# Two planning numbers of a conv and mixer kernel: the second group's convolution counted at 1.2 times its VectorE time, and the decoding of the second token weight put three tenths ahead

## The chip, the cores and the metric

The kernel runs on one core of a Trainium2 chip. The metric is the device time of the program in microseconds. Its engines are called here as the profile calls them: PE (TensorE, matmuls; PEld its weight loads), DVE (VectorE), ACT (ScalarE), POOL (GpSimd) and SP (SyncE, which issues DMAs).

## The reference

Eight batches of 4096 tokens by 192 channels go through a causal convolution of 7 taps, with softmaxed taps for each of 8 heads of 24 channels, and then through a mixer: an MLP over the tokens (4096 to 256 to 4096) and an MLP over the channels (192 to 1536 to 192), each with a residual sum.

```python
w = exp(weight - max); w = w / (sum(w) + 1e-09)          # (8 heads, 7 taps)
x = einsum('hk,bskhg->bshg', w, windows_of_7(x))         # causal, zeros ahead
h = maximum(x^T @ w_tok1, 0) @ w_tok2                    # token mix, for each batch
u = x + h^T
out = u + maximum(u @ w_ch1, 0) @ w_ch2                  # channel mix, for each token
```

The token weights come as pairs of 32-bit words (the two halves of 64-bit floats), so they are decoded on the chip.

## The kernel before

**Groups and tiles.** `GROUPS` has five groups of batches: [0], [1], [2,3], [4,5], [6,7]. While the channel part of one group runs in 8 tiles of 512 tokens, the next group's convolution and first token mix run beside it as background. This document numbers the tiles of group 0 from 0 to 7. In one tile PE does, in program order: `channel1` (L959: six pairs of 18 matmuls into two PSUM tiles, L932; ACT makes `hh` at L971 and DVE `hl` at L972 out of each), `mix2` of the next tile (L861, L862; two DVE sums for each of 4 pieces), half of `channel2` (L1006, L1007), `transposed` of the next tile (L892, copies on ACT L894 and DVE L895), and the other half of `channel2`.

**The background of group 0.** Four lists of items (streams), all of `group=1`:
- the convolution of batch 1 (`stage1(1)`): for each of four quarters of the tokens (`q2`), loads (L621), 8 first taps on ACT (L631) and 48 later taps on DVE (L633), two heads to an item; 96 DVE items in all. A quarter ends with a store on POOL (L657);
- its first token mix (`mix`, L721): 8 items of 4 matmuls for each quarter, which may start when that quarter is convolved;
- the decoding of `w_tok2` (`decode_items`): 12 jobs, each a 512 KB load on SP (L206), an ACT step (L170), four DVE steps (L172, L173, L176, L179), an ACT copy (L185) and a DVE difference (L186). Four jobs make one quarter of `t2s`, which `mix2` of two tiles reads;
- the stores of `t2s`: for each quarter 8 ACT copies into `stage` (L1109, two buffers) and 4 DMAs on SP (L1111) to `t2d`, where later groups read it. Its last item, `through` (L1090), opens the pool for the convolution of group 2 and starts that (`stage1(2)`), with the first of its two halves of channels only; the other half's pool opens after tile 6.

**The planner** (`Background`, L35). The order of all engines is written out while the program is built. Each piece of foreground calls `fg(pe, dve, after)`: it moves a planned PE clock on by `pe` ns, puts background items in until the planned DVE clock is `after` (200 or 600 ns) ahead, and books `dve` ns of foreground. An item moves the planned DVE clock by its `cost`: 660 ns for a pair of taps of batch 1, 3083 ns in all for a decode job. Of the streams whose first item is ready, `fill` (L64) takes the one with the smallest key:

```python
ready = [s for s in ready if s["items"][0].pe]      # once self.dve >= self.pe + until
self.pop(min(ready, key=lambda s: s["done"] / s["total"] - s["lead"]))   # L82
```

So a stream with a lead of 0.1 is kept 0.1 of its own total ahead of one without. Items of cost 0 (loads, ACT steps, stores) also wait while the DVE clock is full. Mix items are left out inside `channel1` (`tiled`). `require` (L94), called before each `mix2` of group 0, puts in whatever of the decoding that tile still needs, and then sets the planned PE clock up to the planned DVE clock. `finish` (L105), called for group 1 at the head of tile 7, puts in all that is left of its four streams.

Of the kernel before, what the change touches and what calls it, by code (L numbers as in the profile page):

```python
# [34 lines left out]
class Background:  # L35
# [9 lines left out]
        self.pe = 0.0  # L45
        self.dve = 0.0

    def add(self, items, lead=0.0, group=None):
        total = sum(it.cost for it in items) or 1.0
        self.streams.append(dict(items=items, total=total, done=0.0, free=self.pe, lead=lead, group=group))  # L50

# [63 lines left out]
def conv_mixer_kernel(ctx: ExitStack, tc: tile.TileContext, x, weight, w_tok1, w_tok2, w_ch1, w_ch2, out):  # L115
# [16 lines left out]
    TT = TJ * P  # L132
# [3 lines left out]

    AHEAD = {1: 5, 2: 3}
    LAST = NJ // MJ - 3
    ST = RB * P

    def f32(ap):
        return ap.bitcast(F32)
# [7 lines left out]
    bg = Background()  # L150
# [94 lines left out]
    def t2_job(q2, a0, na, kc=None):  # L245

        c0 = q2 * ST + a0
        cs = slice(2 * c0, 2 * (c0 + na))
# [22 lines left out]
    def decode_items(dec, jobs, loaded=False):  # L271


        n = dec.n / 0.96
        sts = [{} for _ in jobs]
        items = []

        def add(cost, lag, fn, tag=None, gate=None, eager=False):
            items.append(Item(fn, cost + (190 if cost else 0), lag, gate=gate, tag=tag, eager=eager))

        def load(i):
            def fn():
                jb = sts[i]["jb"] = jobs[i][0]()
                sts[i]["raw"] = jb.get("raw") or dec.load(jb["src"], jb["shape"])

            if i < len(jobs):
                add(0, 0, fn, eager=True)

        def begin(i):
            def fn():  # L290
                sts[i]["a"] = dec.a(sts[i], sts[i]["jb"].get("top", lambda: None)())

            if i < len(jobs):
                add(0, 12e3 if i == 0 and not loaded else 0, fn, eager=loaded and i == 0)

        def high(i):
            if not jobs[i][4]:
                return

            def fn():  # L300
                jb = sts[i]["jb"]
                hi, lo = jb["make"]() if "make" in jb else (jb["hi"], jb["lo"])
                sts[i]["b"] = dec.b(sts[i], hi, lo, jb.get("view", lambda v: v))

            add(0, 0, fn, gate=jobs[i][3])

        def low(i):
            def post():
                if "post" in sts[i]["jb"]:
                    sts[i]["jb"]["post"]()  # L310

            if jobs[i][4]:
                add(n, 0, lambda: sts[i]["b"][0](), jobs[i][1])
            add(0, 0, post, jobs[i][1])
            items.extend(jobs[i][2])

        load(0)
        load(1)
        begin(0)
        for i in range(len(jobs)):  # L320
            if i:
                high(i - 1)
            for k, c in enumerate((0.5, 0.5, 1, 1)):
                add(n * c, 500 if k == 0 else 0, lambda i=i, k=k: sts[i]["a"][k]())
                if k == 0 and i:
                    low(i - 1)
                if k == 2:
                    begin(i + 1)
            load(i + 2)
        high(len(jobs) - 1)  # L330
        add(0, 500, lambda: None)
        low(len(jobs) - 1)
        return items
# [264 lines left out]
    def stage1(gi, pools):  # L598
        bs = GROUPS[gi]
        nb = len(bs)  # L600
        convolving, mixing, accs = [], [], []
# [10 lines left out]
        def load(q2, part):  # L612
# [3 lines left out]
            for i, b in enumerate(bs):  # L616

                at = (b * S + q2 * ST - HALO) * D + ds.start
                assert at >= 0
# [40 lines left out]
        def t1_load(n):  # L660
            q2, q = divmod(n, RB // MJ)
            js = slice(q * MJ, (q + 1) * MJ)

            def part(d):
                return d[q2 * ST:(q2 + 1) * ST].rearrange("(p j) t m -> p j t m", j=RB)[:, js]

            top = t1d.rearrange("s (t m) -> s t m", t=1)
            if nb == 1:
                t1 = mp.tile([P, MJ, 1, JT], F32, name="t1", bufs=AHEAD[nb] + 1)
                nc.sync.dma_start(out=t1, in_=part(top))  # L670
            elif gi == 2:
                if n < LAST:
                    t1 = mp.tile([P, MJ, 2, JT], F32R, name="t1", bufs=AHEAD[nb])
                else:

                    if "spare" not in done:
                        done["spare"] = mp.tile([P, 2, ND, TT], F32R, name="other").rearrange("p a c t -> p (a c t)")
                    w = MJ * 2 * JT
                    t1 = done["spare"][:, (n - LAST) * w:(n - LAST + 1) * w].rearrange("p (j t m) -> p j t m", t=2, m=JT)
                nc.sync.dma_start(out=f32(t1[:, :, 1:2]), in_=part(top))  # L680
            else:
                t1 = mp.tile([P, MJ, 2, JT], F32R, name="t1", bufs=AHEAD[nb])
                nc.sync.dma_start(out=f32(t1), in_=part(t1p))
            states[q2]["t1", q] = t1
            mark("t1", n)
# [5 lines left out]
        def t1_lo(q2, q):  # L691
# [3 lines left out]
            nc.gpsimd.dma_start(  # L695
                out=t1p[q2 * ST:(q2 + 1) * ST].rearrange("(p j) t m -> p j t m", j=RB)[:, js], in_=f32(t1)
            )
# [61 lines left out]
        def multiply(*a):  # L759
# [7 lines left out]
            for kc in range(KC):  # L767
# [3 lines left out]
                mixing.append(it)  # L771
            if n + AHEAD[nb] < (LAST if gi == 2 else NJ // MJ):
                mixing.append(Item(lambda: t1_load(n + AHEAD[nb])))
            if gi == 2 and n % 2 and n // 2 < NJ // MJ - LAST:
                mixing.append(Item(lambda: t1_load(LAST + n // 2)))

# [25 lines left out]
            bg.finish(gi)  # L802
            mix1_done(gi, accs)

        bg.add(convolving, group=gi)
        bg.add(second, group=gi)
        return start, finish

# [5 lines left out]
    def t2s_of(q2):  # L814
        if q2 not in t2s:
            t2s[q2] = t2sp[q2 % 2].tile([P, KC, 2, ST], F32R, name="t2s")
        return t2s[q2]
# [234 lines left out]
    td = decode_ctx.enter_context(tc.tile_pool(name="td", bufs=1, side="right", reuse_waits="tile"))  # L1052
# [5 lines left out]
    def first_items():  # L1058

        jobs, stores = [], []  # L1060
        state = {}

        def decoded(q2):
            state["t2", q2] = max(bg.pe, bg.dve)

        def stored(q2):
            state["stored", q2] = bg.pe

        decoded(0)
        for q2 in range(NS):  # L1070
            for kc in range(KC):
                for r in range(2):
                    a = (q2, kc, r)
                    stores.append(Item(lambda a=a: store_t2(*a, 0), lag=1000, gate=lambda q2=q2: state.get(("t2", q2))))
                    stores.append(Item(lambda a=a: store_t2(*a, 1), lag=600))
                    stores.append(Item(lambda a=a: store_t2(*a, 2), lag=1200))
            stores.append(Item(lambda q2=q2: stored(q2)))
            for a0 in range(0, ST, TT) if q2 else []:
                for kc in range(KC):
                    after = []  # L1080
                    if a0 + TT == ST and kc == KC - 1:
                        after.append(Item(lambda q2=q2: decoded(q2)))

                    def gate(q2=q2):
                        if q2 > 1 and (mixed[0] <= 2 * (q2 - 2) or ("stored", q2 - 2) not in state):
                            return None
                        return 0.0

                    jobs.append((lambda a=(q2, a0, TT, kc): t2_job(*a), ("t2", q2, a0 // TT), after, gate, True))
        def through():  # L1090

            decode_ctx.close()
            conv_pool(0)
            starts[2] = stage1(2, lambda k: cps[k])

        stores.append(Item(through))
        bg.add(decode_items(Decoder(td, TT, 2, 2), jobs), lead=0.1, group=1)
        bg.add(stores, group=1)

    t2p = []  # L1100
# [1 line left out]
    def store_t2(q2, kc, r, step):  # L1102

        if step == 0:
            t2p.append(td.tile([P, 2 * TT], F32R, name="stage", bufs=2).rearrange("m (j p) -> m j p", j=RB))
        if step < 2:
            js = slice(step * RB // 2, (step + 1) * RB // 2)
            v = f32(t2s[q2][:, kc, r]).rearrange("m (p j) -> m j p", j=RB)
            nc.scalar.copy(out=t2p[-1][:, js], in_=v[:, js])  # L1109
        else:  # L1110
            nc.sync.dma_start(out=t2d[q2][:, kc, r], in_=f32(t2p[-1]))  # L1111

    def conv_pool(k):
        cps[k] = ctx.enter_context(tc.tile_pool(name=f"cp{k}", bufs=1, reuse_waits="tile"))

    def run_ahead(gi):

        if gi and gi + 2 < len(GROUPS) and gi + 2 not in starts and bg.idle():
            starts[gi + 2] = stage1(gi + 2, lambda k: cps[k])
# [101 lines left out]
```

## Time and profile before

| | us |
|---|---|
| median of 3 runs (lowest, highest) | 2064.48 (2064.27, 2065.81) |
| the profiled execution's own time | 2064.22 |
| its span in the trace | 2062.5 |
| PE busy (weight loads) | 2051.7 (1898.3) |
| DVE busy | 1402.8 |
| ACT busy | 760.2 |
| granted PE clock, share of full | 1.0 |

The page's first part gives each engine's busy time, the second the same in 40 slices of the span. PE is at nine tenths or more in all of them, DVE in the third to the fifth of them (about 100 to 260 us) too; in the last third of the span DVE is at four to five tenths. A busy PE is not PE at its peak, so tiles are compared by the time from the first matmul of one `channel1` to that of the next: such stretches, and what each engine does in them, come from the view by windows.

### The profile page before, as it was taken

How to read it: one execution, taken by the hardware profiler on the slowest of the kernel's cores; microseconds unless marked ns; L12 is line 12 of the kernel's file. 1: busy time of each engine (PE TensorE's matmuls, PEld its weight loads, DVE VectorE, ACT ScalarE, POOL GpSimd, SP SyncE). 2: the span in 40 equal slices, each digit the busy share in tenths (PEclk: the TensorE clock that was granted, in tenths of full speed). 3: DMA queues.
4: the chain of work that ended last, by engine and by line, in shares of the span. 5: the costliest groups of instructions: out<-in, count | busy, mean ns of one | idle time of the engine just before them, and what ended most of it. 6: DMA issues, size and time to landing. Idle time of an engine off the chain costs nothing.

```text
span 2062.5 us, 41284 instructions
## 1 busy us (share of the span) xinstructions
PE 2051.7 (99%) x17723; PEld 1898.3 (92%) x17723; DVE 1402.8 (68%) x2781; ACT 760.2 (37%) x1305; POOL 101.6 (5%) x167
## 2 busy tenths in 40 slices
PE   9999999999999999999999999999999999999999
PEld 9789999998989989999999999999999999999998
DVE  8799969999569988448965778444445454444444
ACT  4656544434333333223423433233223232233222
POOL 0100000000000000000000000000000000000000
PEclk9999999999999999999999999999999999999999
DMA  9855445554354564232543433322211212222210
GB/s 310 289 164 180 131 135 182 182 174 133 126 169 128 174 172 131 85 96 74 152 125 91 134 125 100 98 60 67 68 45 52 67 48 68 59 67 68 67 32 17
DMA packets 259654, 239.44 MB, mean 116 GB/s; under 512 B 202832, under 2 KB 213584, under 8 KB 257936
## 3 DMA queue, kind: packets, MB, share of 16 engines
q1 hardware_dynamic: 243616, 158.55, 26.7%
q0 software_dynamic: 15856, 78.26, 11.9%
q8 instruction: 140, 2.29, 0.5%
q14 instruction: 42, 0.34, 0.0%
HBM read 146.60 MB, written 71.30 MB: 106 GB/s over the span
## 4 chain that ended last, share of the span: by engine, by line
PE 90%; DVE 8%; ACT 1%; DMA 1%; issue 0%; SPq 0%; POOL 0%; ACTq 0%; POOLq 0%
PE ps_x L932 34%; PE ps_x L1006 16%; PE ps_x L989 16%; PE ps_x L1007 7%; DVE xc L633 3%; PE ps_x L892 2%; PE ps_x L864 2%; DVE hl L972 2%; PE ps_a L725 2%; PE ps_x L866 2%; PE ps_a L727 2%; PE ps_a L726 2%; PE ps_x L865 2%; PE ps_a L426 1%; PE ps_x L861 1%; PE ps_x L495 1%
## 5 line engine op out<-in xcount | busy, mean ns | idle before, releaser
L971 ACT ACTIVATE hh<-ps_x 128x512 fp32r<-128x512 f32 x756 | 411.0, 597 | 808.0 <-PE ps_x L932 808.0
L972 DVE SCALAR_TENSOR_TENSOR hl<-ps_x,hh 128x512 fp32r<-128x512 f32 x756 | 484.8, 684 | 217.6 <-ACT hh L971 216.9
L932 PE MATMUL ps_x<-own,w_hi 64*128 64x512 f32 x2880 | 608.2, 390 | 1.8 <-DVE hl L972 1.3
L1006 PE MATMUL ps_x<-w,hh 128*128 128x384 f32 x1872 | 542.1, 361 | 0.7 <-DVE hl L972 0.7
L932 PEld LDWEIGHTS ps_x<-own,w_hi 64*128 64x128 f32 x2880 | 427.6, 184 | 58.7 <-issue 6.6
L1007 PE MATMUL ps_x<-w,hl 128*128 128x192 f32 x1872 | 468.7, 250 | 0.0
L932 PE MATMUL ps_x<-other,w_hi 64*128 64x512 f32 x1728 | 450.9, 389 | 0.5 <-DVE osb L1011 0.3
L633 DVE SCALAR_TENSOR_TENSOR xc<-raw,cw,xc 128x384 f32<-128x384 f32 (+1 forms) x768 | 388.5, 560 | 9.2 <-ACT xc L631 9.2
L1007 PEld LDWEIGHTS ps_x<-w,hl 128*128 128x128 f32 x1872 | 357.5, 191 | 0.0
L1006 PEld LDWEIGHTS ps_x<-w,hh 128*128 128x128 f32 x1872 | 351.5, 188 | 1.4 <-DVE hl L972 1.3
L932 PEld LDWEIGHTS ps_x<-other,w_hi 64*128 64x128 f32 x1728 | 314.0, 184 | 34.3 <-DVE hl L972 1.9
L989 PE MATMUL ps_x<-w,hh 64*128 64x384 f32 x2304 | 329.9, 355 | 0.0
L932 PE MATMUL ps_x<-own,w_lo 64*128 64x512 f32 x1440 | 326.3, 387 | 0.0
L989 PE MATMUL ps_x<-w,hl 64*128 64x192 f32 x2304 | 292.2, 247 | 0.1
L932 PE MATMUL ps_x<-other,w_lo 64*128 64x512 f32 x864 | 242.1, 386 | 0.0
L932 PEld LDWEIGHTS ps_x<-own,w_lo 64*128 64x128 f32 x1440 | 217.1, 184 | 25.4 <-DVE w_lo L186 0.5
L989 PEld LDWEIGHTS ps_x<-w,hl 64*128 64x128 f32 x2304 | 223.7, 188 | 1.7 <-DVE hl L972 0.8
L989 PEld LDWEIGHTS ps_x<-w,hh 64*128 64x128 f32 x2304 | 219.8, 184 | 0.9
L1010 DVE TENSOR_TENSOR osb<-ps_x,u 128x192 f32<-128x192 f32 x156 | 55.3, 354 | 205.1 <-PE ps_x L1007 204.9
L932 PEld LDWEIGHTS ps_x<-other,w_lo 64*128 64x128 f32 x864 | 159.0, 184 | 16.9
L894 ACT CAST own<-ps_x 128x512 fp32r<-128x512 f32 x120 | 63.2, 593 | 267.8 <-PE ps_x L892 267.6
L997 DVE TENSOR_TENSOR osb<-ps_x,osb 128x192 f32<-128x192 f32 x288 | 103.0, 358 | 17.0 <-PE ps_x L932 0.5
(135 smaller groups left out, 1877.6 us busy)
## 6 DMA issues: line engine op xcount, KB each, us to landing
raw<-in_x_dram SPq DMA_DIRECT2D x56, 672.0 KB, 7.4
t<-t2d SPq DMA_DIRECT2D x64, 512.0 KB, 5.1
out_dram<-osb POOLq DMA_DIRECT2D x63, 384.0 KB, 4.7
u<-xcd SPq DMA_DIRECT2D x62, 384.0 KB, 5.6
xcd<-xc POOLq DMA_DIRECT2D x28, 768.0 KB, 7.4
other<-own POOLq DMA_DIRECT2D x24, 768.0 KB, 5.4
t<-t1p SPq DMA_DIRECT2D x32, 512.0 KB, 4.0
t2d<-stage SPq DMA_DIRECT2D x16, 512.0 KB, 4.0
```

Of the source, the lines that this page charges most:

```text
L633: nc.vector.scalar_tensor_tensor(out=dst, in0=src, scalar=cw[:, h, k:k + 1], in1=dst, op0=ALU.mult, op1=ALU.add)
L725: nc.tensor.matmul(out=ps, lhsT=wh, rhs=xh, start=a, stop=False)
L726: nc.tensor.matmul(out=ps, lhsT=wh, rhs=xl, start=False, stop=False)
L894: nc.scalar.copy(out=own[:, 0, c], in_=ps)
L932: nc.tensor.matmul(out=ps, lhsT=w1[w][rows, c, p * P:(p + 1) * P], rhs=t[h][rows, v, c], start=n == 0, stop=n == len(prods) - 1,)
L971: nc.scalar.activation(out=h["hh", f], in_=ps, func=AF.Relu)
L972: nc.vector.scalar_tensor_tensor(out=h["hl", f], in0=ps, scalar=0.0, in1=f32(h["hh", f]), op0=ALU.max, op1=ALU.subtract)
L989: nc.tensor.matmul(out=ps[:, :m], lhsT=h[part, f][ks, ts], rhs=w2[ks, f, :m], start=n == 0 and part == "hh", stop=z and part == "hl",)
L997: nc.vector.tensor_tensor(out=osb[:, j], in0=v, in1=osb[:, j], op=ALU.add)
L1006: nc.tensor.matmul(out=ps[:, :2 * D], lhsT=h["hh", f][:, ts], rhs=w2[:, f, :], start=n == 0, stop=False)
L1007: nc.tensor.matmul(out=ps[:, :D], lhsT=h["hl", f][:, ts], rhs=w2[:, f, :D], start=False, stop=z)
L1010: nc.vector.tensor_tensor(out=rows(osb[:, j]), in0=rows(ps[:, :D]), in1=tokens(u, i)[:, j], op=ALU.add)
```

## The change

`add` takes a factor `pace` by which the costs of a stream's items are multiplied. The convolution of group 1 is added with 1.2, so a pair of its taps counts 792 ns instead of 660 on the planned DVE clock; all others are added with 1.0. The decoding of `w_tok2` gets a lead of 0.3 instead of 0.1. No instruction is added, removed or changed in shape; the order in which the planner puts them in differs.

```diff
-    def add(self, items, lead=0.0, group=None):
+    def add(self, items, lead=0.0, group=None, pace=1.0):
+
+        for it in items:
+            it.cost *= pace
         total = sum(it.cost for it in items) or 1.0
...
+    PACE = 1.2
...
-        bg.add(convolving, group=gi)
+        bg.add(convolving, group=gi, pace=PACE if gi == 1 else 1.0)
         bg.add(second, group=gi)
...
-        bg.add(decode_items(Decoder(td, TT, 2, 2), jobs), lead=0.1, group=1)
+        bg.add(decode_items(Decoder(td, TT, 2, 2), jobs), lead=0.3, group=1)
         bg.add(stores, group=1)
```

## Rows read from the trace of the kernel before

**Rows 1.** Part 1 of the page (busy us, share of the span, instructions)

```profile
PE 2051.7 (99%) x17723; PEld 1898.3 (92%) x17723; DVE 1402.8 (68%) x2781; ACT 760.2 (37%) x1305; POOL 101.6 (5%) x167
```

**Rows 2.** Windows by tile, tiles 1 to 6 (PE, PEld, DVE, ACT, POOL, clock, DMA)

```profile
98.61:130.52 31.91, 30.97 (x233) 27.77 (x233) 31.28 (x78) 21.27 (x38) 0.75 (x1) 1.00 0.45 146
130.52:166.11 35.59, 35.59 (x266) 32.60 (x266) 35.28 (x89) 23.43 (x40) 1.31 (x2) 1.00 0.65 194
166.11:201.37 35.26, 35.26 (x265) 32.49 (x264) 34.95 (x89) 19.12 (x35) 1.31 (x2) 1.00 0.51 149
201.37:237.55 36.18, 35.49 (x265) 34.06 (x264) 35.27 (x89) 19.17 (x36) 1.31 (x2) 1.00 0.61 190
237.55:272.73 35.18, 35.18 (x265) 33.50 (x264) 25.20 (x63) 19.33 (x30) 1.71 (x3) 1.00 0.45 144
272.73:302.70 29.97, 29.97 (x235) 28.91 (x234) 26.57 (x55) 11.86 (x25) 1.45 (x3) 1.00 0.20 63
```

**Rows 3.** Windows of line L633 on DVE, tiles 1, 2, 4 and 6

```profile
98.61:130.52 31.91, 12.08 (x34) 1.00 0.45 146
130.52:166.11 35.59, 15.27 (x44) 1.00 0.65 194
201.37:237.55 36.18, 15.27 (x44) 1.00 0.61 190
272.73:302.70 29.97, 12.90 (x24) 1.00 0.20 63
```

**Rows 4.** Windows of line L186 on DVE, tiles 1, 3 and 4

```profile
98.61:130.52 31.91, 2.06 (x3) 1.00 0.45 146
166.11:201.37 35.26, 1.36 (x2) 1.00 0.51 149
201.37:237.55 36.18, 2.06 (x3) 1.00 0.61 190
```

**Rows 5.** Timeline of DVE in channel1 of tile 2 (start, us, what)

```profile
133.82 2.06 DVE L633 SCALAR_TENSOR_TENSOR xc<-raw,cw,xc 128x192 f32<-128x192 f32 x6
135.79 1.28 DVE L972 SCALAR_TENSOR_TENSOR hl<-ps_x,hh 128x512 fp32r<-128x512 f32 x2
136.99 0.42 DVE L172 TENSOR_SCALAR dec_top<-dec_top 128x512 f32<-128x512 f32 x1
137.32 1.28 DVE L972 SCALAR_TENSOR_TENSOR hl<-ps_x,hh 128x512 fp32r<-128x512 f32 x2
```

**Rows 6.** Windows of line L1109 on ACT, channel1 of tiles 1, 2, 4

```profile
98.61:111.10 12.49, 6.04 (x5) 1.00 0.69 231
130.52:143.50 12.98, 0.00 (x0) 1.00 0.35 102
201.37:213.90 12.53, 3.96 (x4) 1.00 0.94 282
```

**Rows 7.** Timelines of ACT and PE, tile 1, and of ACT, tile 4

```profile
102.65 1.12 ACT L971 ACTIVATE hh<-ps_x 128x512 fp32r<-128x512 f32 x2
103.61 1.28 ACT L1109 CAST stage<-t2s 128x512 fp32r<-128x512 f32 x1
...
106.16 1.56 PE L932 MATMUL ps_x<-own,w_hi 64*128 64x512 f32 x6 [0.84 <-DVE hl L972]
...
212.09 1.19 ACT L1109 CAST stage<-t2s 128x512 fp32r<-128x512 f32 x1 [1.00 <-DMA t2d<-stage]
```

**Rows 8.** Timelines of DVE, PE, SP and DVE, tiles 5 and 6

```profile
256.74 2.06 DVE L633 SCALAR_TENSOR_TENSOR xc<-raw,cw,xc 128x192 f32<-128x192 f32 x6
...
264.53 1.47 PE L721 MATMUL ps_a<-xc,t 128*128 128x192 f32 x8
...
265.01 1.89 SPq L621 DMA_DIRECT2D raw<-in_x_dram  x2
...
278.99 1.14 DVE L633 SCALAR_TENSOR_TENSOR xc<-raw,cw,xc 128x384 f32<-128x384 f32 x2
```

**Rows 9.** View of tile dec_raw, 80 to 270 us

```profile
DMA to landing us min/median/max: 3.5/4.0/8.9
```

## The prediction

> **What bounds the kernel now.** I read the page first: PE is busy for 2051.7 of 2062.5 us [rows 1], so whatever the planner's two numbers can win is time that PE spends waiting in the stretch which they touch. That stretch is tiles 1 to 6 of group 0: the convolution of batch 1 and the decoding run there and nowhere else. So the next view is the windows by tile [rows 2]. Tile 6 has no mix matmuls and takes 29.97 us; tile 5 has 32 of them and takes 35.18, so these cost 5.21 us and a full tile is 29.97 or 35.18 us of plain PE work. Against that the lengths show the waiting: tile 1 31.91 - 29.97 = 1.94 us; tiles 2 to 4 0.41, 0.08 and 1.00 over 35.18; tiles 5 and 6 none. Together 3.43 us, 0.17% of the kernel. This is the pot.
>
> The busy columns would tell other sums. PE's own column shows a loss of 0.94 and 0.69 us alone, in tiles 1 and 4. The weight loads, by contrast, fill 28.91 of 29.97 us in tile 6 (96.5%) but less in tiles 1 to 4: 126.92 us of loads in all [rows 2], which at 96.5% would fit into 131.5 us, 7.4 us less than the 138.94 us that these tiles take. I go by the lengths: tile 5 has 1.01 us more of weight loads than tile 3 for the same work and is 0.08 us shorter, so that column moves without the time. The Trainium skill (Perfetto Trace Analysis, "Identifying the Most-Contended Engine") holds matmul busy time to be a poor measure of headroom and takes the share of weight loads instead; the first half agrees with these rows, by the second half the pot would be the 7.4 us.
>
> What does PE wait for? In tiles 1 to 4 DVE is busy for 31.28 of 31.91, 35.28 of 35.59, 34.95 of 35.26 and 35.27 of 36.18 us: full [rows 2]. But that alone cost 0.08 us in tile 3. The two tiles that lose are those where ACT's copies for the transposed store fall into `channel1`: five in tile 1 and four in tile 4, none in tile 2 [rows 6]; each takes 1.2 us, and can stand 1.00 us waiting for its buffer's DMA with all of ACT behind it. In tile 1 the first pair's `hh` starts at 102.65 us, 4 us into the tile, the second is behind a copy at 103.61, and PE waits 0.84 us for an `hl` at 106.16 [rows 7]. So a full DVE costs little by itself, and a full DVE plus a late ACT costs 1 to 2 us a tile.
>
> **The change part by part.** Nothing is removed or added; 192 tap instructions, 12 decode jobs and 32 store copies are put elsewhere.
>
> *How much the planner puts in now.* Tap pairs count 0.66 us, jobs 3.08. Tiles 2 to 4 hold 44, 45 and 44 taps ([rows 3]; tile 3 is left out there), 66.5 pairs or 43.9 us, and eight jobs (three, two, three) [rows 4], 24.6 us: 22.8 us counted a tile. Tile 1, without mix matmuls, holds 17 pairs and three jobs, of which I take the first as mostly done before: about 19. A later tile without mix gets 22.8 - 5.1 = 17.7 (a mix item counts 0.64, eight make 5.1).
>
> *The pace.* The convolution counts 96 x 0.79 = 76 us instead of 63, so both streams are 113 instead of 100 us, and the planner needs half a tile more. What DVE really does per counted microsecond falls: a tap takes 0.33 us ((135.79 - 133.82) / 6), a two-operand step 0.60, a short one 0.33 [rows 5], so a job is 2 x 0.33 + 3 x 0.60 = 2.46.
>
> *The lead.* Decoding goes first until it is 0.3 done, then both advance together: 113 us for a whole of each. From about 0.07 done at 98.6 us: tile 1 spends 8.5 us on that, the other 10.5 move both by 0.093, so it ends with convolution 0.09 and decoding 0.39 (before 0.18 and about 0.27). Tile 2: +0.16, so 0.25; the first quarter is ready only at its end, and its 5.21 us of mix matmuls move to tile 3, at no cost to PE's sum. Tile 3: 0.45; tile 4: 0.65; in tile 5 the decoding ends at 0.70, then 18 us go to taps alone: 0.94. Tile 6 has 4.5 us counted, six pairs, left. Before, the last taps ran at 256.74 us, in tile 5 [rows 8].
>
> *What that does to DVE.* Tile 6 before shows the foreground: 26.57 - 12.90 of taps = 13.67 us [rows 2, 3]. Tile 1 after: 13.67 + 0.09 x 192 x 0.33 + 0.32 x 12 x 2.46 = 28.8 of 29.97 us. Tiles 3 and 4: 13.67 + 0.20 x (63.4 + 29.5) = 32.3 of 35.18. DVE is no longer full anywhere in tiles 1 to 5.
>
> *What that does to ACT.* Each quarter's copies follow the last of its four jobs, so they move with the decoding. Decoding 0.33 falls at about 120 us, late in tile 1; the copies run 11 us at least and two or three may reach `channel1` of tile 2, which had none. Decoding 0.67 falls in `channel2` of tile 3, so the four copies in `channel1` of tile 4 move ahead of it. Those in tile 1 follow the weight decoded before and stay. Hence I give tile 1 a remaining loss of 1.0 us (bounds 0 and 1.94, what five copies cost with a full DVE; halfway, as the copies stay and DVE is 93 to 96% full), and tiles 2 to 5 0.5 together (bounds 0 and 1.94, all of tile 1's loss once more).
>
> *The end of the stage.* The loads, decode steps and stores pass no other queue's items than before but earlier; each load waits on SP for its buffer as now. The mix of the last quarter moves to tile 6 or to `finish` at tile 7's head. If the last taps come only there, PE waits for DVE's queue: 0 where tile 6 takes all, about 1.0 for one or two pairs plus DVE's lag; I take 0.5. Group 2's first half of taps (24 of them, 12.90 us in tile 6 [rows 3]) still fits, as tile 7 has room, and later groups go on as before.
>
> *Sum.* After: 1.0 + 0.5 + 0.5 = 2.0 of waiting instead of 3.43: 1.4 us less. The profiled execution took 2064.22 us, 0.26 below the median of the runs, so it is as good a base: 2064.2 - 1.4 = **2062.8 us**. By the bounds of the terms alone: 2060.8 (nothing waits) to 2064.2 + (1.94 + 1.94 + 1.0 - 3.43) = 2065.7.
>
> **The rivals.**
>
> *No gain: the copies only move.* Two quarters' copies land on `channel1` of tiles 2 and 4 and cost there what they did in tiles 1 and 4. For it: the planner knows nothing of ACT. Against it: DVE is emptier. Time 2064.2, up to 2066.
>
> *Slower: group 1's convolution is overtaken.* When the stores end, group 2's convolution joins at key 0, ahead of a convolution at 0.9. Before, its loads went at 265.01 us and its taps began at 278.99, 14 us later, with group 1's long done at 259 [rows 8]. Now group 1's remainder competes in tile 6, where 29.97 - 13.67 - 12.90 = 3.4 us of DVE are free [rows 2, 3]. If more than that is left when group 2's taps begin, the rest goes in at `finish`, with the last 32 mix matmuls, and PE, in order, waits. My six pairs take 4 us, most of them before that point; if tiles 1 to 5 each take 2 us less than I counted, 10 us more are left, some 6 us over after tile 6, 5 real; with DVE's lag of 1.5 the wait is 6.5 us: 2062.8 + 6.5 = 2069.3. It decides from about 6 us counted left at that point.
>
> *No gain or worse: decoding outruns its loads.* A load takes 4.0 us, 3.5 to 8.9 [rows 9], and only two buffers exist. With decoding first, a job in `channel2` takes some 4.3 us of plan, and from a load's issue to the ACT step that reads it there are some 2.5; ACT then stands 1.5 us, for three or four jobs. What stands behind on ACT are the `hh` of the next `channel1` and the copies of `transposed`; those have 7 us to spare in `channel2`. Time 2064 to 2067. The Trainium skill (TensorE: Matmul & The Clock Gate, "Architectural detail: the array is 16× 32×32, not 1× 128×128") has ACT's and DVE's queues strictly in order, which is what makes such a wait reach PE; the copy that stands 1.00 us in tile 4 [rows 7] agrees.
>
> *Far faster.* If the weight loads' share were the measure, up to 7.4 us: 2056.8. Nothing in the lengths backs it.
>
> *It does not do what it says.* If loads or gates, not the key, set the decoding's pace, the order hardly changes: 2064.2.
>
> **How the numbers follow.** What a measurement can tell here is 0.2%, 4.1 us: faster is below 2060.4, slower above 2068.6. Chances: forecast 0.52 (2061 to 2064), copies only move 0.20, loads 0.06, no change 0.02, overtaken 0.13, far faster 0.07. Of the overtaken case a quarter stays below 2068.6, and I add 0.03 of slower for what I don't see: faster 0.07, same 0.80, slower 0.13. The range reaches from the forecast's lower bound to the lesser half of the overtaken case: 2060.5 to 2067.5.
>
> **What would show it.** Right: tile 1 at 30 to 31 us with some 18 taps instead of 34, tile 2 near 30 without mix matmuls, the first `L721` in tile 3, tile 4 without copies in its `channel1` and at 35.2 us, taps of group 1 in tile 6, tile lengths from group 1 on unchanged. Wrong: taps of group 1 behind tile 6's last matmul with PE idle there; copies in `channel1` of tile 2 with a tile above 31 us; ACT idle ahead of L170; or a change of length after 333 us, which I hold to be none.

## The result, and the profile after

The changed kernel takes 2070.52 us (median; 2069.85 to 2073.0), the kernel before 2064.60 us in the same comparison. The ratio is 1.003 with a 95% interval of 1.0019 to 1.004: **slower by 5.9 us**, where 2062.8 us and no change that a measurement can tell had been forecast. The profiled execution took 2071.13 us; its span is 2069.3 us, against 2062.5 before. The names of lines shift by four (by six in the runs with the edit of e1, below): the taps are L637, the mix matmuls L725, `channel1` L936, `hl` L976, `dec_top` L174, the copies into `stage` L1113.

The page's first part hardly shows it; it answers to [rows 1]:

```profile
PE 2053.1 (99%) x17723; PEld 1895.6 (92%) x17723; DVE 1404.9 (68%) x2781; ACT 759.8 (37%) x1305; POOL 101.5 (5%) x167
```

The windows by tile do. These are tiles 1 to 6 of group 0, as in [rows 2], with the same columns (length, then busy time and instructions of PE, PEld, DVE, ACT and POOL, the clock, the DMA share and GB/s):

```profile
100.28:132.82 32.54, 31.27 (x234) 27.83 (x233) 30.67 (x70) 22.52 (x38) 0.75 (x1) 1.00 0.40 124
132.82:162.72 29.90, 29.90 (x234) 27.30 (x233) 28.71 (x71) 20.23 (x35) 1.17 (x2) 1.00 0.51 171
162.72:197.82 35.10, 35.10 (x266) 32.50 (x265) 33.59 (x83) 19.43 (x36) 0.89 (x2) 1.00 0.62 175
197.82:232.92 35.10, 35.10 (x266) 32.50 (x265) 32.12 (x79) 18.44 (x35) 1.30 (x2) 1.00 0.51 164
232.92:268.05 35.13, 35.13 (x267) 32.45 (x266) 32.24 (x83) 21.52 (x36) 1.30 (x2) 1.00 0.47 144
268.05:309.20 41.15, 37.01 (x266) 35.65 (x266) 33.94 (x78) 11.79 (x24) 3.14 (x5) 0.96 0.32 95
```

Tiles 2 to 5 are at plain work: 29.9 us without mix matmuls, 35.1 with 32 of them. Tile 6 now holds 32 mix matmuls (266 PE instructions instead of 235) and should take 35.1 too; it takes 41.15, and its clock is 0.96. Against the kernel before (in whose trace these six tiles take 31.91, 35.59, 35.26, 36.18, 35.18 and 29.97, with the mix matmuls elsewhere) tile 1 loses 0.6 us, tiles 2 to 5 win 1.8, and tile 6 loses 6.0 that it shouldn't. Together that is 4.9 us. Tile 0 was 1.7 us longer as well, with the same order of instructions; a second execution of the kernel before had that too (below), so I take it for chance. From tile 7 on the lengths are those of before.

Where tile 6 loses it, three views tell. First what PE waits for in that tile (engine, line waited for: us in total, times, longest):

```profile
PE ps_a L725 <- DVE xc L637: 4.1, 1, 4.1
```

A mix matmul waits for a tap. Then the timelines of DVE and PE at the end of the tile (start, us, what, idle before and releaser); `128x384` are taps of group 2, `128x192` those of group 1:

```profile
278.58 1.14 DVE L637 SCALAR_TENSOR_TENSOR xc<-raw,cw,xc 128x384 f32<-128x384 f32 x2
...
297.95 2.86 DVE L637 SCALAR_TENSOR_TENSOR xc<-raw,cw,xc 128x384 f32<-128x384 f32 x6
300.72 0.35 DVE L1014 TENSOR_TENSOR osb<-ps_x,u 128x192 f32<-128x192 f32 x1
301.11 0.36 DVE L1015 TENSOR_TENSOR osb<-ps_x,osb 128x192 f32<-128x192 f32 x1
301.38 0.74 DVE L637 SCALAR_TENSOR_TENSOR xc<-raw,cw,xc 128x192 f32<-128x192 f32 x2
...
302.18 7.09 PE L725 MATMUL ps_a<-xc,t 128*128 128x192 f32 x32 [4.14 <-DVE xc L637]
```

Group 2's 24 taps begin at 278.58 us, and the last pair of group 1 runs at 301.38, behind all of them; the pair before it is in the group of six at 297.95, whose other four are group 2's (such a pair takes 0.74 us, and four taps of group 2 2.20). PE ended `channel2` at 298.04. DVE takes up that last result only at 300.72: it is 2.7 us behind PE. PE stands until 302.18, when the last pair is done. So of the 4.1 us some 1.4 are the two pairs' own work, and the rest is what stood ahead of them. Third, the windows of that end:

```profile
292.00:298.04 6.04, 6.04 (x43) 5.80 (x42) 5.97 (x14) 0.00 (x0) 0.00 (x0) 1.00 0.00 0
298.04:302.18 4.14, 0.01 (x1) 0.01 (x1) 4.04 (x10) 0.00 (x0) 0.42 (x1) 0.99 0.00 0
302.18:305.60 3.42, 3.42 (x11) 3.42 (x12) 0.00 (x0) 0.00 (x0) 0.87 (x2) 0.51 0.72 260
305.60:309.20 3.60, 3.60 (x24) 3.38 (x23) 0.18 (x1) 0.33 (x1) 0.00 (x0) 1.00 0.22 85
```

After 4.14 us without work PE runs at 0.51 for 3.4 us, which is the lower of its two levels, 1.2 GHz. The 32 mix matmuls take 7.0 us from 302.18 to the next `channel1`; in a kernel shown below, at full clock, 5.4. So 6.0 us are 4.1 of waiting and 1.6 of slow clock, and 0.3 are spread over the tile. The Trainium skill (TensorE: Matmul & The Clock Gate, "HAM oscillation — how this bites in real kernels") tells that a wait for data lets the gate drop the clock, and that the work behind it starts at the low rate; this trace agrees, with 0.51 behind one such wait.

The small loss of tile 1 stands in the timelines of ACT and PE there:

```profile
103.27 0.68 ACT L174 ACTIVATE dec_top<-dec_raw 128x512 f32<-128x512 f32 x1 [2.45 <-DMA dec_raw<-in_moe_w_tok_dram]
104.30 0.62 ACT L189 CAST t2s<-dec_top 128x512 fp32r<-128x512 f32 x1 [0.35 <-DVE dec_top L183]
104.82 1.22 ACT L1113 CAST stage<-t2s 128x512 fp32r<-128x512 f32 x1
105.93 0.81 ACT L635 ACTIVATE xc<-raw,cw 128x192 f32<-128x192 f32 x2
106.63 3.03 ACT L975 ACTIVATE hh<-ps_x 128x512 fp32r<-128x512 f32 x6
...
108.00 1.56 PE L936 MATMUL ps_x<-own,w_hi 64*128 64x512 f32 x6 [1.09 <-DVE hl L976]
```

ACT stands 2.45 us for a decode load, the first `hh` comes 6.35 us into the tile (4.0 before, [rows 7]), and PE waits 1.09 us for an `hl`.

### The profile page after: what moved, and what is told of

Read it like the earlier page. It is cut to its first block, busy times and chain, and to the rows that moved or that the text cites. A ratio compares the mean times of both kernels' runs of the same rounds, so it can differ in the third digit from the quotient of the medians.

```text
span 2069.3 us, 41277 instructions
## 1 busy us (share of the span) xinstructions
PE 2053.1 (99%) x17723; PEld 1895.6 (92%) x17723; DVE 1404.9 (68%) x2781; ACT 759.8 (37%) x1305; POOL 101.5 (5%) x167
## 4 chain that ended last, share of the span: by engine, by line
PE 91%; DVE 5%; DMA 2%; ACT 1%; SPq 1%; issue 0%; DVEq 0%; ACTq 0%
PE ps_x L936 35%; PE ps_x L1010 17%; PE ps_x L993 16%; PE ps_x L1011 8%; PE ps_x L896 2%; DVE xc L637 2%; PE ps_x L868 2%; PE ps_a L729 2%; PE ps_x L870 2%; PE ps_a L731 2%; PE ps_a L730 2%; PE ps_x L869 2%; DMA dec_raw<-in_moe_w_tok_dram 2%; DVE hl L976 1%; PE ps_a L430 1%; PE ps_x L865 1%
## 5 line engine op out<-in xcount | busy, mean ns | idle before, releaser
L976 DVE SCALAR_TENSOR_TENSOR hl<-ps_x,hh 128x512 fp32r<-128x512 f32 x756 | 484.9, 685 | 221.0 <-ACT hh L975 220.0
L936 PE MATMUL ps_x<-own,w_hi 64*128 64x512 f32 x2880 | 606.3, 390 | 2.2 <-DVE hl L976 1.4
L936 PEld LDWEIGHTS ps_x<-own,w_hi 64*128 64x128 f32 x2880 | 423.2, 184 | 62.3 <-issue 6.3
L936 PE MATMUL ps_x<-other,w_hi 64*128 64x512 f32 x1728 | 451.0, 389 | 0.5 <-DVE osb L1015 0.3
L637 DVE SCALAR_TENSOR_TENSOR xc<-raw,cw,xc 128x384 f32<-128x384 f32 (+1 forms) x768 | 388.2, 561 | 11.3 <-ACT xc L635 11.3
L936 PEld LDWEIGHTS ps_x<-other,w_hi 64*128 64x128 f32 x1728 | 314.0, 184 | 32.9 <-DVE hl L976 1.9
L936 PE MATMUL ps_x<-own,w_lo 64*128 64x512 f32 x1440 | 324.9, 387 | 0.0
L936 PE MATMUL ps_x<-other,w_lo 64*128 64x512 f32 x864 | 242.1, 386 | 0.0
L936 PEld LDWEIGHTS ps_x<-own,w_lo 64*128 64x128 f32 x1440 | 214.6, 184 | 27.3 <-DVE w_lo L190 0.5
L936 PEld LDWEIGHTS ps_x<-other,w_lo 64*128 64x128 f32 x864 | 159.0, 184 | 16.1
```

Of the source, the lines that this page charges most:

```text
L637: nc.vector.scalar_tensor_tensor(out=dst, in0=src, scalar=cw[:, h, k:k + 1], in1=dst, op0=ALU.mult, op1=ALU.add)
L936: nc.tensor.matmul(out=ps, lhsT=w1[w][rows, c, p * P:(p + 1) * P], rhs=t[h][rows, v, c], start=n == 0, stop=n == len(prods) - 1,)
L976: nc.vector.scalar_tensor_tensor(out=h["hl", f], in0=ps, scalar=0.0, in1=f32(h["hh", f]), op0=ALU.max, op1=ALU.subtract)
```

## The experiments

The theory after this reading: **the remainder is overtaken**. The two new numbers remove the waits of tiles 2 to 5 as forecast, but they leave two pairs of group 1's taps for the time after group 2's convolution has joined with key 0; those pairs end behind it on a full DVE, and the last mix matmuls wait. Rivals: the pace or the lead costs something of its own elsewhere; or the price is the pairs' own work, not DVE's backlog. Each time is given with the difference to the runs of the kernel before in the same comparison.

**Group 2 last (e1).** The change as it is, but group 2's convolution is added one whole unit behind the others, until `finish`.

```diff
     def finish(self, group=None):
         mine = [s for s in self.streams if s["group"] == group]
+        for s in self.streams:
+            s["lead"] = max(s["lead"], 0.0)
...
-        bg.add(convolving, group=gi, pace=PACE if gi == 1 else 1.0)
+        bg.add(convolving, group=gi, pace=PACE if gi == 1 else 1.0, lead=-1.0 if gi == 2 else 0.0)
```

> The changed kernel with one more edit: group 2's convolution gets a lead of -1 until group 1 is finished, so it can't be taken ahead of group 1's. In the changed kernel tile 6 and the turn to tile 7 take 41.15 us, 6.0 more than plain work, of which PE stands 4.14 us behind DVE's taps. Overtaken: the last taps and the 32 mix matmuls come before group 2's taps, the wait goes, tile 6 takes 35.2 us, and the kernel 2070.5 - 6.0 = 2064.5 us. No room: DVE has too much to do in tile 6 in whatever order, the wait stays or moves, 2069 to 2071 us. Loads: what the change costs lies in tiles 0 and 1 (1.7 and 0.6 us more than before), then 2070 us less whatever tile 6 gives, with tile 1 still at 32.5 us.

Measured: 2064.09 us, ratio 0.9994 (0.9986 to 1.0003), 1.4 us below before. That is the first of the three forecasts. Its windows of tile 6, and DVE's timeline inside that tile and at its end:

```profile
267.64:302.76 35.12, 35.12 (x265) 34.06 (x265) 33.30 (x76) 12.12 (x26) 2.45 (x4) 1.00 0.41 130
```
```profile
280.19 0.75 DVE L639 SCALAR_TENSOR_TENSOR xc<-raw,cw,xc 128x192 f32<-128x192 f32 x2
...
282.05 1.14 DVE L639 SCALAR_TENSOR_TENSOR xc<-raw,cw,xc 128x384 f32<-128x384 f32 x2
...
302.87 0.36 DVE L1016 TENSOR_TENSOR osb<-ps_x,u 128x192 f32<-128x192 f32 x1 [1.65 <-PE ps_x L1013]
```

The tile is at plain work and the clock is full. All 24 taps of group 2 still run in this tile, but behind group 1's last pair at 280.19, and the last 32 mix matmuls stand inside `channel2`. DVE is as busy as in the changed kernel (33.30 and 33.94 us), but here it waits for PE at the end instead of PE for it. So the loss was the order of the two streams, and with it the place of those matmuls. Tiles 1 to 6 together take 202.6 us, against 204.0 in the trace of before.

**Pace alone (e2), lead alone (e5).** One number of the change each: `lead` back at 0.1, and `PACE` at 1.0.

```diff
-        bg.add(decode_items(Decoder(td, TT, 2, 2), jobs), lead=0.3, group=1)
+        bg.add(decode_items(Decoder(td, TT, 2, 2), jobs), lead=0.1, group=1)
```

> Only the pace of 1.2; the decoding keeps its lead of 0.1. Overtaken: the stores end later, group 2's convolution starts later, behind group 1's last taps (in the built order its first 6 taps stand behind transposed of tile 6), so no wait at the turn, and DVE is not full in tiles 2 to 5: 2070.5 - 6.0 - 0.6 = 2063.9 us or a little less. If the pace by itself is what costs: 2068 or more. Loads: tile 1 back to 32 us or less, as the decoding no longer runs ahead of its loads.

Measured: 2070.17 us, 1.0023 (1.0014 to 1.0032), 4.7 us slower. That wasn't expected: by the number it is the forecast for a pace that costs by itself. Tile 1 is at 31.2 us, but tile 2, with 32 mix matmuls, takes 39.27 instead of 35.1. PE's timeline there, and windows from 143.5 us on, the last of them of the slow stretch alone:

```profile
146.85 0.36 PE L866 MATMUL ps_x<-h,t2s 128*128 128x192 f32 x1 [2.28 <-DVE t2s L190]
```
```profile
143.50:150.00 6.50, 4.22 (x22) 3.63 (x19) 5.99 (x16) 2.15 (x5) 0.00 (x0) 0.83 0.01 3
150.00:156.00 6.00, 6.00 (x40) 6.00 (x39) 4.91 (x14) 5.40 (x9) 0.55 (x1) 0.90 0.60 161
...
147.80:151.25 3.45, 3.45 (x15) 3.45 (x15) 3.03 (x10) 1.71 (x5) 0.00 (x0) 0.51 0.02 5
```

With the convolution counted dearer and no greater lead the decoding is late for the `mix2` of tile 3, which `require` calls for; PE waits 2.28 us and then again runs at the lower clock. So the lead pays for the pace: it cures a wait that the pace alone would make. That is not all of the 4.7 us. From tile 7 on this run takes 1762.6 us, where the kernel before takes 1760.1 (e6, below), and 2.0 of these 2.5 us are a wait for `t<-t2d` at 482 us, behind tile 6 by 176 us. There SP issues the loads of `t2d` behind two loads of `raw` that go out at 467.00 us, in the changed kernel at 461.23; whether they are late because group 2's convolution started late isn't shown. The kernel with the `finish` behind, below, has this wait too.

```diff
-    PACE = 1.2
+    PACE = 1.0
```

> Only the lead of 0.3; the convolution counts 1.0. In the built order group 2's convolution is also taken ahead (16 taps in tile 5), but group 1's last taps stand in tile 5 and its last mix matmuls in channel2 of tile 6, with no mix at the turn. Overtaken, with the wait only where PE has nothing between: no wait at the turn, 2064 to 2065 us, as before. If taking group 2 ahead costs by itself: 2067 or more. Loads (decoding ahead of its loads): tile 1 at 32.2 us or more as in the changed kernel, and the kernel 1 us over what tiles 2 to 5 win.

Measured: 2067.62 us, 1.0011 (1.0003 to 1.002), 2.7 us slower: the forecast "taking group 2 ahead costs by itself". Tile 5, with 48 mix matmuls, takes 38.3 us and tile 6, with 16, 35.36 where 32.5 is plain (tiles 2 and 3 of this run, with 16 each). ACT and DVE at the head of tile 6, then PE:

```profile
268.44 2.13 ACT L635 ACTIVATE xc<-raw,cw 128x384 f32<-128x384 f32 x4 [6.85 <-POOL raw L627]
269.09 6.44 DVE L637 SCALAR_TENSOR_TENSOR xc<-raw,cw,xc 128x384 f32<-128x384 f32 x12 [1.86 <-ACT xc L635]
275.45 0.35 DVE L1014 TENSOR_TENSOR osb<-ps_x,u 128x192 f32<-128x192 f32 x1
...
276.34 0.93 PE L936 MATMUL ps_x<-own,w_hi 64*128 64x512 f32 x5 [1.20 <-DVE osb L1015]
```

DVE stands 1.86 us for the first tap on ACT, which itself had waited for POOL's write into the new `raw` tile; then twelve taps of group 2 run in a row, 6.4 us of work, ahead of `osb` and `hl`. This is a second way to lose with group 2's convolution: not that it overtakes taps, but that it comes in one piece ahead of foreground.

**Two other paces (e3: 1.3, e7: 1.1).** Both change only the number.

> The changed kernel with a pace of 1.3: in the built order three pairs of taps are left for the turn instead of one or two, and group 2 has 16 of its taps in front of them instead of 24. If the wait is what DVE still has before it when PE comes to the mix matmuls, it is about the same, 4 us, and the kernel takes 2070 to 2071 us. If each pair left over has its price (4.1 us for two), 6 us or more, and 2072.5 us.

Measured: 2069.32 us, 1.0019 (1.001 to 1.0028), 3.9 us slower, below both forecasts. Three pairs are left now instead of two, and the wait is shorter. What PE waits for, and DVE's last taps ahead of the turn:

```profile
PE ps_a L725 <- DVE xc L637: 2.8, 1, 2.8
...
297.19 2.05 DVE L637 SCALAR_TENSOR_TENSOR xc<-raw,cw,xc 128x192 f32<-128x192 f32 x6
```

So the price isn't one for each pair. Here group 2 has eight taps in front, not 16, and DVE isn't behind: it takes up PE's last result at once, and the three pairs themselves are 2.05 of the 2.8 us. The wait is all that DVE still has to do, up to the end of the last pair, when PE comes.

> The changed kernel with a pace of 1.1. In the built order 18 taps of group 2 still stand ahead of group 1's last pair in tile 6, but that pair comes ahead of the second half of channel2 and the 32 mix matmuls inside it. If the place of the last taps against the turn decides, and not the overtaking: no wait, 2070.5 - 6.0 = 2064.5 us. If overtaking decides: 2068 or more.

Measured: 2068.03 us, 1.0014 (1.0005 to 1.0023), 3.1 us slower, so the first forecast fell: there is no wait at the turn (the mix matmuls wait 0.3 us for a tap), but tile 6 takes 38.18 us all the same, 3.1 over plain work. Of these only 1.0 is idle time of PE:

```profile
268.97:307.15 38.18, 37.16 (x266) 32.80 (x265) 29.95 (x65) 11.69 (x25) 1.31 (x2) 1.00 0.15 49
```

PE's busy column holds 2.1 us above plain work, at full clock: stalls that the profile books as busy. Group 2's first taps come at the head of `channel1` here, with DVE behind; e9, below, tests whether their overtaking is what costs.

**Group 2 last, with other numbers (e8, e9, e10, e11).** The edit of e1, and with it: pace 1.1 and lead 0.2 (e8), pace 1.1 (e9), pace 1.0 (e10), lead 0.2 (e11).

> Group 2's convolution last, pace 1.1, lead 0.2: the decoding is 3 jobs, not 4, in tile 1. If ACT standing for loads of the decoding makes the loss of tile 1 (2.45 us of wait in the changed kernel, tile 1 32.5 us), tile 1 comes to 31 to 31.5 us and the kernel to 2063.0 us; if the three copies of the store in channel1 make it, tile 1 comes to no less than 32 and the kernel stays at 2064.1, as with group 2 last alone.

Measured: 2064.67 us, 0.9997 (0.9988 to 1.0006), 0.3 us below before. This doesn't decide about tile 1. It takes 31.86 us, between the two forecasts, but the run did not take the cause away: four jobs still end in the tile, and ACT stands 2.4 us for a load as before. Tile 3, with 16 mix matmuls, loses 1.2 us (33.66).

> Pace 1.1 and lead 0.3 as in the run with pace 1.1 alone (2068.0 us, tile 6 38.2 us with 35.2 of plain work), with group 2's convolution last until group 1 is finished. In the built order six taps of group 2 still stand at the end of tile 5 and eight in channel1 of tile 6 (ten before), but group 1's last pair and its mix matmuls come ahead of them. Overtaken: tile 6 comes to 35.2 us and the kernel to 2065.0 us. If group 2's taps in channel1 of tile 6 fill DVE and hold PE up, whatever they overtake: tile 6 stays above 37 us, the kernel at 2067 to 2068.

Measured: 2067.52 us, 1.0013 (1.0004 to 1.0022), 2.3 us slower; tile 6 takes 37.41 us. So most of the loss at pace 1.1 isn't overtaking, or e1's edit would have cured it. DVE and PE at the head of tile 6:

```profile
273.04 3.26 DVE L639 SCALAR_TENSOR_TENSOR xc<-raw,cw,xc 128x384 f32<-128x384 f32 x6
276.22 2.48 DVE L978 SCALAR_TENSOR_TENSOR hl<-ps_x,hh 128x512 fp32r<-128x512 f32 x4
...
276.96 1.56 PE L938 MATMUL ps_x<-own,w_hi 64*128 64x512 f32 x6 [1.38 <-DVE hl L978]
```

Group 1's taps are all put in in time, and so group 2's follow at once: six of them stand ahead of `hl` on a DVE that is already behind. That these six are the cause is read from the timeline; no run moved them alone.

> Lead 0.3 alone with group 2's convolution last. Lead alone took 2067.6 us, with 2.8 us lost in tile 6 (35.4 us, 32.6 of plain work) and as much in tile 1. Here eight taps of group 2 stand in channel1 of tile 6 as there, 12 in tile 5 instead of 16. Overtaken: 2.8 us come back, 2064.8. Full DVE by group 2's taps in channel1: 2067 to 2068.

Measured: 2065.53 us, 1.0001 (0.9992 to 1.001), as before; tile 6 is 0.7 us above plain work instead of the 2.8 of e5. Group 2's taps still come at its head, but eight in a row instead of twelve, and `osb` follows at 273.25 us instead of 275.45; PE waits for neither.

> Group 2's convolution last, pace 1.2, lead 0.2. Tile 6 has no tap of group 2 in channel1, so 35.2 us there by both theories. Decoding has three jobs instead of four in tile 1: by the theory that ACT standing for its loads makes tile 1 slow, tile 1 31.2 to 31.9 us instead of 32.2 and the kernel 2063.5; the decoding must not be late for tiles 2 to 4, else one of them is above 36 us.

Measured: 2063.94 us, 0.9993 (0.9984 to 1.0002), 1.3 us below before, all of tiles 2 to 6 at plain work. Tile 1 takes 32.0 us; here too four jobs end in it and ACT stands 2.2 us for a load, so the theory on the loads is as untested as in e8. This run and e1 are the best found; the interval of neither excludes no change.

**Keep PE busy through the wait (e4).** 24 transposes of the identity, of no use to the result, stand on PE ahead of the last mix matmuls.

```diff
         def finish():
+            if gi == 1:
+                ps = ps_x.tile([P, TT], F32, name="ps_x")
+                for k in range(24):
+                    nc.tensor.transpose(out=ps[:, k % TJ * P:(k % TJ + 1) * P], in_=ident, identity=ident)
             bg.finish(gi)
```

> The changed kernel with 24 transposes of nothing on PE ahead of the last mix matmuls, 24 x 0.162 = 3.9 us, where PE stands idle for 4.14 us. Behind that wait the granted clock is 0.51 for 3.4 us and the 32 matmuls take 7.0 us instead of 5.2. If the idle time is what lowers the clock, the 1.8 us come back: 2068.7 us and a clock of 1.00 there. If the matmuls are slow for another reason (their weights, a load): 2070.5 us.

Measured: 2068.55 us, 1.0016 (1.0007 to 1.0025), 3.1 us above before instead of 5.9. PE's timeline at the end of tile 6:

```profile
296.91 2.78 PE L809 MATMUL ps_x<-ident 128*128 128x128 f32 x24
301.33 5.47 PE L725 MATMUL ps_a<-xc,t 128*128 128x192 f32 x32 [1.63 <-DVE xc L637]
```

and the windows of tile 6:

```profile
267.09:306.72 39.63, 38.00 (x289) 36.64 (x288) 34.05 (x79) 11.82 (x25) 3.14 (x5) 1.00 0.34 99
```

The taps come no sooner, but the mix matmuls behind them take 5.47 us instead of 7.09, and the clock is 1.00 throughout the tile. With added work the tile is 1.5 us shorter (39.63 for 41.15): the slow clock was a price of the idle time, about 1.6 us, and a part of its own.

**The `finish` behind `channel1` of tile 7 (e12).** Group 1's remainder and the last mix matmuls are put behind `channel1` of tile 7, so that DVE has 12.5 us more.

```diff
+                if ahead and gi == 0:
+                    h = channel1(abc[i])
                 if turn and nxt[0] != gi:
                     starts[nxt[0]][1]()
...
                     loaded = load_tile(*nxt, sp)
                 if ahead:
-                    h = channel1(abc[i])
+                    if gi:
+                        h = channel1(abc[i])
```

> The changed kernel with the end of group 1's stage (its last taps, 32 mix matmuls) put behind channel1 of tile 7 instead of ahead of it. All of DVE's order up to there is as in the changed kernel, group 2 still ahead of group 1's last pair. If PE's order at the turn is what turns DVE's lag into a wait: DVE has 12.5 us to come up, the wait of 4.14 us and the slow clock go, about 1 us comes for h1 right ahead of mix2: 2070.5 - 6.0 + 1.0 = 2065.5 us. If DVE's lag itself delays PE in tile 6 or 7: channel1 of tile 7 takes the wait, 2068 to 2070 us.

Measured: 2075.16 us, 1.0047 (1.0034 to 1.0061), 10 us slower. The wait for the taps is gone and tile 6 is at plain work, but tile 7 takes 43.68 us. Timelines of PE and SP, and the windows there:

```profile
309.18 5.47 PE L725 MATMUL ps_a<-xc,t 128*128 128x192 f32 x32
314.68 0.88 SPq L831 DMA_DIRECT2D t<-t2d  x2
318.58 0.41 PE L865 MATMUL ps_x<-h,t 128*128 128x384 f32 x1 [3.93 <-DMA t<-t2d]
```
```profile
316.00:322.00 6.00, 2.20 (x9) 2.03 (x9) 0.17 (x1) 0.00 (x0) 0.00 (x0) 0.82 1.04 308
322.00:328.00 6.00, 6.00 (x29) 6.00 (x28) 2.60 (x8) 1.41 (x4) 1.14 (x2) 0.61 1.12 306
```

A new wait took the place of the old one: the loads of `t2d` for the next group moved with the `finish` and go out only at 314.68 us, when the last mix matmul is done and right where `mix2` needs them; PE waits 3.9 and 1.2 us, and the clock falls again, to 0.82 and 0.61 in the two windows. So this run doesn't say what the move alone is worth.

**The kernel before once more (e6).** One profiled execution, for tile 0 and the spread of the tiles.

> The kernel before once more, for its tile 0. Up to there it has the same order of instructions as the changed kernel, but tile 0 took 37.7 us in the profile of before and 39.4 after. If that is chance from one execution to the next, tile 0 lies here between 37.5 and 39.5 us, likely above 38; if the change makes it, again at 37.7.

Measured: tile 0 39.4 us (37.7 in the first trace), tiles 1 to 6 204.0 us together, as in the first trace. Tiles 2 to 4:

```profile
131.40:166.94 35.54, 35.54 (x266) 32.60 (x266) 34.64 (x87) 22.91 (x39) 1.31 (x2) 1.00 0.66 197
166.94:202.90 35.96, 35.91 (x266) 32.59 (x266) 35.65 (x91) 19.95 (x38) 1.31 (x2) 1.00 0.49 144
202.90:238.93 36.03, 35.38 (x266) 34.04 (x266) 35.18 (x89) 19.03 (x36) 1.31 (x2) 1.00 0.61 190
```

Tile 0's length changes from execution to execution, so its 1.7 us are no effect of the change. Tile 3 takes 35.96 us here and 35.26 in [rows 2].

## Why the prediction was wrong

**The pot, and what the tile lengths measure.** Right. Plain work is 29.9 and 35.1 us, and in the changed kernel and in e1, e4 and e12, with the same order there, tiles 2 to 5 sit on it. The weight loads as a measure of what is left fell with that: tiles 5 before and 3 after, both with 32 mix matmuls and at plain work, have 33.50 and 32.50 us of loads in 35.18 and 35.10 us.

**The planner's course.** Right to a few taps in tiles 1 to 4, and short in tile 5. Forecast were 17, 31, 38, 38 and 56 taps in tiles 1 to 5 (0.94 - 0.65 of 192 in the last); the windows of the taps' line show 19, 30, 40, 36 and 49. A part of that is the sum itself: 22.8 us less the 5.65 in which the decoding ends leaves 17.2 us in tile 5, not 18, and seven pairs over instead of six. The mix of the first quarter moved to tile 3 (first L725 at 175.86 us), tile 2 lost its mix matmuls, and nothing changed from tile 7 on.

**ACT's copies.** The explanation isn't borne out, though the sum that stood on it came out. I had a full DVE cost little alone and 1 to 2 us with copies in `channel1`. But tiles lose with a full DVE and no copy: 0.9 us in tile 3 of e6 and in tile 3 of e7 (DVE busy for 35.24 of 35.97 us there). So the 35.26 us of tile 3, from which I argued, was one execution of two. And four copies in `channel1` cost nothing in tiles 2 and 4 of the changed kernel (3.87 and 4.11 us of them; those of tile 4 didn't move ahead), with DVE busy for 28.71 of 29.90 and 32.12 of 35.10 us. But DVE isn't the whole of it either. These are tiles 2 and 3 of e5, with four copies and none, both at plain work:

```profile
132.13:164.66 32.53, 32.53 (x250) 29.86 (x250) 31.70 (x79) 21.31 (x35) 1.31 (x2) 1.00 0.54 172
164.66:197.14 32.48, 32.48 (x251) 31.21 (x250) 32.14 (x81) 21.21 (x35) 0.76 (x1) 1.00 0.65 201
```

DVE is as full there as in tiles 2 to 4 of the kernel before. So neither a busy share nor the copies tell when a tile loses. What made tiles 2 to 4 lose before stays open; no run changed it by itself.

**Tile 1.** Mis-sized: I took a loss of 1.0 us and it is 2.6 (32.54 - 29.9). The rival "decoding outruns its loads" is what I had put at 0.06, with 1.5 us of ACT standing; it stands 2.45 us. The number of jobs was right (four for 3.8 counted). That the late load is the price is argued, from the timelines of ACT and PE and from e2: there, with the lead at 0.1, three jobs end in the tile, no load is late by more than 0.7 us, and it takes 31.2 us with all five copies in its `channel1`. But 33 taps run in that tile instead of 19, so the late load isn't tested alone; e8 and e11 kept it.

**Tiles 2 to 5.** I took 0.5 us of loss; it is none. e1, where the next term is gone, shows the two together: tile 1 at 32.24 us is 0.3 above the trace of before, tiles 2 to 6 are 1.8 below, 1.45 in all. Too little for tile 1 and too much for the others met in a gain that was the forecast's, 1.4: that is luck.

**The end of the stage.** This is the step that failed: 0.5 us taken, 1.0 as its bound, 6.0 measured. I had the remainder too small, but that matters little (12 taps for tile 6; it was 20, of which the last four count), the place right ("the rest goes in at `finish`, with the last 32 mix matmuls, and PE, in order, waits"), and as a rival even the price: 6.5 us, of which 6.0 came. What was wrong is the condition, "it decides from about 6 us counted left at that point". Two pairs, 1.6 us counted, were left when group 2's taps began, and that was enough. The condition asked whether the tile has free DVE time for the remainder. But a stream with key 0 doesn't share with one at 0.98: all 12 pairs of group 2 go first, whatever is free in the sum, and then DVE's whole lag stands in front of the last pair. I put that lag at 1.5 us; it was 2.7, and 1.5 more passed until the last pair was done. The prediction's own list of signs against it had this one: "taps of group 1 behind tile 6's last matmul with PE idle there". With "any remainder is overtaken" as the condition, and a remainder forecast in the main line itself, this rival would have been the forecast, and not a case of chance 0.13.

**What I left out.** The clock. The wait of 4.14 us at this place costs 1.6 us more behind it (e4). My 6.5 met the 6.0 partly by chance: I had 5 us of taps and 1.5 of lag, and it was 4.1 of DVE's queue and 1.6 of clock.

**The two numbers.** I costed them as one and they pull apart: alone the pace makes the decoding late (e2, +4.7, of which 2.5 lie behind tile 6), the lead alone brings group 2's taps in one piece (e5, +2.7). Only with group 2 held behind group 1 is the 1.4 us seen (e1; its interval doesn't exclude none), and for pace 1.1 with lead 0.3 not even then (e9).

## What to carry to other kernels

Where streams share an engine by their done shares, ask at each place where a new stream joins what is left of the old ones: a share has no deadline, and a remainder of 2% waits behind all of the newcomer. The last piece of work that gates an in-order engine needs a rule of its own (e1), and its price if late is not its own length alone: the backlog of the engine that makes it comes on top (2.7 us here), and the slow clock behind the wait (1.6). Moving that point later (e12) moves everything that stood with it, loads too.

## What the runs showed of the hardware

A single wait was enough for the clock: 4.14 us idle was followed by 0.51 for 3.4 us, a wait of 2.28 us (e2) by 0.51 too, and waits of 3.93 and 1.22 us (e12) by a window at 0.61. One of 1.63 us right behind 2.78 us of transposes (e4) left it at 1.00. PE's busy column can hide stalls: tile 6 at pace 1.1 shows 37.16 us busy at full clock for work that takes 35.1 elsewhere. And a stage whose instructions stand in the same order can take 37.7 or 39.4 us (tile 0), more than this change's whole gain would have been.
